# Transposing K and Q of the later batches with the DMA crossbar instead of TensorE, in a block-sparse attention and GELU kernel

## The chip, the cores and the metric

The kernel runs on one core of one Trainium2 chip. The metric is device time in microseconds (us) of one execution; medians are over the executions of one kernel on one chip. Each variant ran in the same rounds as the kernel before, on the same chip. A ratio is the mean time of one kernel's fast runs over the mean of the other's fast runs of the same rounds, so it is not quite the ratio of the medians that are quoted. Faster or slower needs 2%.

## The reference, cut to what matters

```python
# q, k, v: (4, 8, 768, 64) fp32; block 32, so 24 blocks; 3 sampled blocks for each query block
mask = |blk_i - blk_j| <= 1, or either of them the first or last block, or blk_j sampled for blk_i
attn = softmax(where(mask, q @ k.T / 8, -1e9)) @ v       # per batch and head
x = attn as (3072, 512)
out = gelu(x @ w_in) @ w_out                             # 512 -> 2048 -> 512, gelu with erf
```

Batch 0 computes dense scores with a mask; batches 1 to 3 gather sampled keys and values per query block.

## The kernel before

The work is a pipeline of half batches (384 rows each). In the stretch that I call a half, TensorE (PE) runs the hidden layer ("H" in the order strings) and the output layer ("O") of one half batch, and between them the scores ("S") and weighted sums ("W") of the next one. A fixed string of tokens gives the order of issue, and every engine takes its instructions in that order.

For batches 1 to 3, GpSimd's (Pool's) queue loads K and Q and converts them to bf16 on the way. TensorE transposes each head pair into PSUM, and VectorE (DVE) copies the result to SBUF:

```python
def load_qk(b, which, n):                       # four heads at once, bf16 tile
    t = st_pool.tile([P, NPAIR, NT * D], BF16, tag="st", name="st")
    pool.dma_start(out=t, in_=src[b, 4 * n:4 * n + 4].rearrange("h (p j) d -> p h (j d)", j=NT))

def transpose_qk(b, hp, which, pair, eng, st):  # 12 transposes, one copy
    dst = qkt_pool.tile([P, S], BF16, tag=f"t{which}", name=f"t{which}")
    ps = home[0].tile([P, NT, P], BF16, tag=home[1], name="ps")
    for j in range(NT):
        for h in range(2):
            pe.transpose(ps[64 * h:64 * h + 64, j, :], pair[:, h, j * D:j * D + D], ident)
    ...                                         # cuts: copy ps -> dst on VectorE
```

V is loaded in fp32 (batch 1 from Pool's queue, the others from SyncE's (SP's)) and cast by VectorE (`own_step`, token "B"). Then six SBUF-to-SBUF transfers on SyncE's queue move its blocks into four rotated copies (`rotate_all`, token "R"). Pool gathers the sampled values from these (`gather_v`, token "C", tile `v_gat`) and the sampled keys (`gather_k`, token "K", tile `kg_all`).

The softmax here doesn't subtract the row's maximum and nothing guards it: scores larger than these inputs give would overflow.

Of the kernel before, what the change touches and what calls it, by code (L numbers as in the profile page):

```python
# [19 lines left out]
P = 128  # L20
# [17 lines left out]
NROT, NULL, NAT1 = NT, NB, NB + 1  # L38
# [21 lines left out]
A0 F00 k1 F01 F02 q1 F03 F04 F05 k3 P0 F10 F11 F12 k2 q2 F13 J0 F14 F15 F20 V00 V01 V02 F21 J1 F22 q3 F23 F24 F25 X0 F30 V10 V11 V12 P1 F31 F32 J2 F33 X1 V20 V21 V22 J3 F34 M1 F35 X2 V30 V31 L1 V32 H X3"""  # L60
FIRST = """
H H m0 I0 m1 m2 I1 H H m3 m4 H I2 I3 H H I4 H O2 I5 O1 f00 O2 f01 m5 f02 O2 I6 I7 F03 F04 V00 O1 F05 f10 V01 O1 f11 V02 f12 f13 O2 f14 f15 O1 V10 O1 X0 F20 F21 u0 V11 V12 B F22 F23 V20 O1 t0 f24 f25 O1 X1 V21 O1 f30 F31 u1 V22 F32 O2 t1 f33 F34 O1 V30 f35 K00 X2 O1 I8 O1 V31 V32 Q0 O1 R Q1 H K01 X3 O2"""
SECOND = """
H t2 H u3 t3 C00 H C01 C02 H G H H H M2 H K02 O2 K03 S0 u2 K11 K10 C10 C11 O4 D0 O2 L2 W0 S1 O3 D1 X0 C12 O1 E0 W1 S2 O2 E1 O1 X1 K12 D2 O1 W2 S3 O2 X2 E2 D3 O1 W3 E3 O2 K13 Y X3 O3 H"""
SPARSE = """
H H Z H H B H O1 H H O1 H O2 S0 O1 t1 K01 O3 W0 S1 O1 t0 X0 O2 W1 u0 S2 X1 O1 K00 R O2 C00 O1 C01 C02 u1 W2 S3 O2 X2 O3 W3 H O2 X3 O2"""
DENSE = """
M3 H H t2 u2 H H H t3 u3 H H H O2 K03 K02 O1 L3 K10 S0 O1 C10 O2 D0 O1 G O1 W0 S1 O1 K12 O2 C11 D1 O1 X0 W1 C12 S2 O2 E0 K13 O1 D2 O1 E1 W2 S3 O1 K11 O1 X1 E2 D3 O1 W3 E3 O2 Y X2 O3 X3 H"""
SPARSE2 = """
H H Z H H B H O1 H H O1 H O2 S0 O1 t1 K01 O3 W0 S1 O1 t0 X0 O2 W1 u0 S2 X1 O1 K00 R O2 C00 O1 C01 C02 u1 W2 S3 O2 X2 O3 W3 H O2 X3 O2"""  # L70
DENSE2 = """
H H t2 u2 H H H t3 u3 H H H O2 K03 K02 O1 K10 S0 O1 C10 O2 D0 O1 G O1 W0 S1 O1 K12 O2 C11 D1 O1 X0 W1 C12 S2 O2 E0 K13 O1 D2 O1 E1 W2 S3 O1 K11 O1 X1 E2 D3 O1 W3 E3 O2 Y X2 O3 X3 H"""
LAST_SPARSE = """
H H H Z H O1 H H H H O2 S0 O5 S1 W0 O5 W1 S2 O1 X0 X1 O3 W2 S3 O4 X2 O1 W3 H X3 O2"""
LAST = """
H H H O2 H H O2 H H H O28"""
# [4 lines left out]
def kernel(  # L81
# [23 lines left out]
    sc_pool, og_pool, mm_pool = psum(opening, 0, (3, 1, 1))  # L105
    st_pool = ctx.enter_context(tc.tile_pool(name="st_pool", bufs=4))
# [21 lines left out]
    def load_v(b, eng):  # L128

        t = stv_pool.tile([P, NT, H, D], F32, tag="st_v", name="st_v")  # L130
        for n in range(NT):
            eng.dma_start(out=t[:, n], in_=v[b, :, n * P:n * P + P].rearrange("h p d -> p h d"))
        return t
# [51 lines left out]

    kg_all = small("kg_all", [2, NPAIR, NQH, P], BF16, const)
# [23 lines left out]
    qgl = [small(f"qgl{hp}", [P], BF16, const) for hp in range(NPAIR)]  # L210
    vgl = [small(f"vgl{i}", [NPAIR, 2 * VW], BF16, const) for i in range(2)]
    n_all = (NAT1 + NT) * H * GW
    v_flat = small("v_flat", [2 * -(-n_all // DW) * DW], BF16, const)
# [8 lines left out]
    pe.matmul(ps_raw, lhsT=ones, rhs=raw_b, start=True, stop=True)  # L222
    dve.tensor_copy(sbf.rearrange("p n s -> p (n s)"), ps_raw)
    dve.tensor_scalar(hit, sbf, key_b[:, 0:1], None, op0=ALU.is_equal)
    for s in range(NR):
        dve.tensor_add(seen, seen, hit[:, :, s])
    dve.tensor_scalar(barred.rearrange("p (n c) -> p n c", c=BLOCK),
                      seen.unsqueeze(2).to_broadcast([P, NB, BLOCK]),
                      0.5, -30000.0, op0=ALU.is_lt, op1=ALU.mult)
# [31 lines left out]
    dve.memset(v_own[0][:, :, :, D:2 * GW], 1.0)  # L261

    def first_own(hp):
        r = slice(2 * hp, 2 * hp + 2)
        dve.tensor_copy(v_own[0][:, :, r, 0:D],
                        first_v[:, r].rearrange("p h (j d) -> p j h d", d=D))

    def gather_constants():
        dve.tensor_copy(sbi, sbf)

        for n, (m, op) in enumerate(((15, ALU.bitwise_and), (7, ALU.bitwise_and),
                                     (8, ALU.bitwise_and), (5, ALU.arith_shift_right))):
            dve.tensor_single_scalar(lane_i[:, n:n + 1], part_i, m, op=op)
        dve.tensor_copy(lane, lane_i)
        dve.tensor_single_scalar(lane[:, 1:2], lane[:, 1:2], float(GW), op=ALU.mult)
        dve.tensor_single_scalar(lane[:, 2:3], lane[:, 2:3], 0.125, op=ALU.mult)
        for s in range(NR):
            dve.tensor_single_scalar(slotm[:, s:s + 1], lane[:, 3:4], float(s), op=ALU.is_equal)

        dve.tensor_scalar(mask_ka, mask_ka, lane[:, 0:1], None, op0=ALU.is_equal)  # L280
        dve.tensor_scalar(rowm, rowm, lane[:, 0:1], None, op0=ALU.is_equal)

        for h, picks in enumerate((((2, 1), (3, 0)), ((0, 8), (3, 13)))):
            (a0, add0), (a1, add1) = picks
            dve.tensor_scalar(base_k[:, h, :], cols, float(add0), rowm[:, a0:a0 + 1],
                              op0=ALU.add, op1=ALU.mult)
            dve.tensor_scalar(term, cols, float(add1), rowm[:, a1:a1 + 1],
                              op0=ALU.add, op1=ALU.mult)
            dve.tensor_add(base_k[:, h, :], base_k[:, h, :], term)
        dve.memset(v_flat[:, 2 * NULL * H * GW:2 * n_even * DW], 0.0)  # L290
        if 2 * n_all < v_flat.shape[1]:
            dve.memset(v_flat[:, 2 * n_all:], 0.0)
        dve.memset(v_own[1][:, :, :, D:2 * GW], 1.0)
# [58 lines left out]
    def value_indices(par, eng):  # L352

        if par:
            own = msk.tile([P, NQ], F32, name="own")
            eng.tensor_scalar(own, base_v, float(NROT) - 0.5, float(NAT1),
                              op0=ALU.is_lt, op1=ALU.mult)
            eng.tensor_add(base_v, base_v, own)
        for h in range(2):
            even = base_v[:, NQH * h:NQH * h + NQH:2]  # L360
            eng.tensor_sub(step, base_v[:, NQH * h + 1:NQH * h + NQH:2], even[:, 0:5])
            eng.tensor_copy(idx_vf[:, h, :], even)
            eng.tensor_scalar(step, step, lane[:, 2:3], None, op0=ALU.mult)
            eng.tensor_add(idx_vf[:, h, 0:5], idx_vf[:, h, 0:5], step)
        eng.tensor_scalar(idx_vf, idx_vf, float(H * GW), lane[:, 1:2], op0=ALU.mult, op1=ALU.add)
        eng.tensor_copy(idx_v[par], idx_vf)
# [22 lines left out]
    def own_v(b, st_v, lo, hi, eng):  # L389
        n = slice(lo, hi)  # L390
        cast(eng, v_own[b % 2][:, n, :, 0:D], st_v[:, n])
# [16 lines left out]
    def gather_v(b, hb, c):  # L408
# [3 lines left out]
            v_flat.bitcast(F32)[:, 0:n_even * DW if b % 2 == 0 else None]  # L412
# [21 lines left out]
    def globals_qk(b, hp, which, eng, st):  # L434
        gl = kgl[b % 2][hp] if which == "k" else qgl[hp]
        for i in range(2):
            rs = slice(64 * i, 64 * i + 64)
            cast(eng, gl[rs, rs].rearrange("p (n c) -> p n c", n=2),
                 st[which, hp][rs, :].rearrange("p (n c) -> p n c", c=BLOCK)[:, 0::NB - 1, :])
# [40 lines left out]
    def dense_scores(hp, st):  # L480

        pd = p_pool.tile([P, NT, P], BF16, tag="pd", name="pd")
        sd = sc_pool.tile([P, 2, 512], F32, tag="sc", name="sd")
        for t in range(NT):
            pe.matmul(sd[:, t // 3, t % 3 * P:t % 3 * P + P], lhsT=st["k", hp][:, t * P:t * P + P],
                      rhs=qgl[hp], start=True, stop=True)
        act.activation(pd.rearrange("p (a t) c -> p a (t c)", a=2), sd[:, :, 0:3 * P],
                       AF.Exp, scale=scale)
        st["pd", hp] = pd
# [89 lines left out]

    def pair_x(hb, hp, og, st):  # L580
# [26 lines left out]
    def hidden_steps(b, hb, st):  # L607
# [12 lines left out]
        def gelu(m):  # L620
            if m == 0:
                st["g", hb] = g_pool.tile([P, KOUT, HALF], BF16, tag="g", name="g")
            act.activation(st["g", hb][:, m:m + 2, :], held.pop(m)[:, :, 0:HALF], AF.Gelu)
# [5 lines left out]
        def step(m):  # L629
            mms(m, range(KIN - 1, KIN) if m < 4 else range(KIN))  # L630
            gelu(m)
# [35 lines left out]
    def first_pair(hp, which="kq"):  # L667
        for w in which:
            pair = st["st", w, hp // 2][:, 2 * (hp % 2):2 * (hp % 2) + 2, :]
            if hp == 0:  # L670
                cast(act if w == "k" else dve, pair, first_st[w])
# [5 lines left out]
    def load_batch(b):  # L677
        for n in range(2):
            for w in "kq":
                sts[b]["st", w, n] = load_qk(b, w, n)  # L680

    def transpose_next(b, hp, w):
        transpose_qk(b, hp, w, sts[b]["st", w, hp // 2][:, 2 * (hp % 2):2 * (hp % 2) + 2, :],
                     dve, sts[b])
        globals_qk(b, hp, w, pool, sts[b])
# [13 lines left out]
    def fetch_v(b):  # L699
        sts[b]["st", "v"] = load_v(b, pool if b == 1 else sp)  # L700

    def clear_keys():
        for t in kgl[0] + kgl[1] + qgl:
# [25 lines left out]
    def run(half, order):  # L729
# [5 lines left out]
        if nb < B:  # L735
# [19 lines left out]
            "t": lambda hp: transpose_next(b + 1, hp, "k"),  # L755
            "u": lambda hp: transpose_next(b + 1, hp, "q"),
# [5 lines left out]
            "L": lambda n: load_batch(n),  # L762
            "M": lambda n: fetch_v(n),
# [45 lines left out]
```

## Time and profile before

| | |
|---|---|
| time | 288.87 us, median of 3 runs (287.73 to 289.42); with the fourth run of the result's rounds 288.30 |
| profiled run | span 286.8 us, granted TensorE clock 1.0 |
| PE busy | 93% |
| all DMA queues | 49.9% of the 16 engines' time, see below |

To see where time goes, I cut each trace at the starts of ScalarE's (ACT's) table loads that precede the gelus of a half, as its timeline shows them. Before, in us: opening 29.6, then eight halves of 45.7, 27.4, 30.5, 32.2, 31.7, 33.0, 29.4 and 27.2.

### The profile page before, as it was taken

The numbers are of one execution on the slowest core, as the hardware profiler recorded it, in microseconds if no ns is written. First come the engines' busy times: TensorE is split into PE (matmuls) and PEld (weight loads), VectorE is DVE, ScalarE is ACT, GpSimd is POOL, SyncE is SP. The second block draws the span as 40 slices with busy tenths as digits, with TensorE's granted clock in tenths as the row PEclk, the third lists the DMA queues.
The fourth block names the chain that finished last, engine by engine and source line by source line (L and its number), as shares of the span: only waits on it lengthen the run. The fifth ranks groups of instructions, "written<-read, shape, count | busy, mean of one in ns | idle before, by whom it ended". The sixth has DMA issues, their size and how long they took to land.

```text
span 286.8 us, 7929 instructions
## 1 busy us (share of the span) xinstructions
PE 265.4 (93%) x3453; PEld 163.5 (57%) x3495; DVE 142.0 (50%) x375; ACT 162.5 (57%) x215; POOL 95.1 (33%) x134
## 2 busy tenths in 40 slices
PE   1999799999799999999999999999998999999995
PEld 1466454465456765566566755566555755565544
DVE  7255498898804670486325652465326560153002
ACT  3698558774367555744467635654466635845420
POOL 8400830013444336334273534231453333100000
PEclk9999999999999999999999999999999999999999
DMA  7999999209891003969580970088000100000101
GB/s 167 238 250 209 209 234 201 58 2 237 219 181 39 11 33 70 186 155 257 128 137 37 135 163 2 3 201 217 37 2 37 41 37 2 25 35 19 39 37 73
DMA packets 30036, 31.27 MB, mean 109 GB/s; under 512 B 13649, under 2 KB 24146, under 8 KB 30002
## 3 DMA queue, kind: packets, MB, share of 16 engines
q0 software_dynamic: 11936, 13.24, 26.5%
q1 hardware_dynamic: 18064, 17.53, 23.4%
q8 instruction: 27, 0.44, 0.6%
q14 instruction: 7, 0.06, 0.1%
q10 hardware_dynamic: 2, 0.00, 0.0%
HBM read 27.26 MB, written 6.29 MB: 117 GB/s over the span
## 4 chain that ended last, share of the span: by engine, by line
PE 60%; DVE 16%; issue 11%; POOL 7%; ACT 5%; POOLq 0%; DVEq 0%; ACTq 0%
PE hp L54 21%; PE op L54 18%; PE s L54 7%; PE og L54 6%; PE ps L54 4%; POOL kg_all L54 3%; POOL v_gat L54 2%; DVE v_flat L54 2%; PE psx L54 2%; DVE v_gat L54 1%; ACT L54 1%; ACT g L54 1%; POOL st L54 1%; PE od L54 1%; ACT kg_all L54 1%
## 5 line engine op out<-in xcount | busy, mean ns | idle before, releaser
L54 PE MATMUL op<-w_out_sb,g 128*128 128x512 bf16 (+1 forms) x358 | 89.8, 370 | 2.2 <-issue 0.2
L54 PE MATMUL hp<-xT,w_in_sb 128*128 128x384 bf16 x512 | 88.5, 326 | 2.9 <-ACT g L54 2.5
L54 ACT ACTIVATE g<-hp 128x768 bf16<-128x768 f32 x64 | 51.0, 810 | 61.1 <-PE hp L54 61.0
L54 PEld LDWEIGHTS <-w_in_sb 128*128 128x128 bf16 x512 | 49.1, 98 | 38.3 <-issue 5.2
L54 ACT ACTIVATE pt_all<-s 128x1024 bf16<-128x1024 f32 (+2 forms) x72 | 44.2, 687 | 30.4 <-PE s L54 30.3
L54 PEld LDWEIGHTS <-g 128*128 128x128 bf16 x400 | 35.6, 98 | 27.4 <-issue 1.6
L54 POOL INDIRECT_COPY kg_all<-tk,idx_k 128x704 f32 x24 | 30.3, 1262 | 58.8 <-issue 53.9
L54 DVE TENSOR_TENSOR pt_all<-pt_all,mask_x 128x768 bf16<-128x768 bf16 x24 | 14.7, 614 | 56.5 <-ACT pt_all L54 56.5
L54 POOL INDIRECT_COPY v_gat<-v_flat,idx_v 128x1024 f32 (+1 forms) x18 | 28.5, 1581 | 39.7 <-issue 16.4
L54 DVE COPY os<-op 128x512 f32<-128x512 f32 (+1 forms) x25 | 16.7, 667 | 21.5 <-PE op L54 20.9
L54 PEld LDWEIGHTS <-pt_all 128*32 128x32 bf16 (+2 forms) x818 | 22.0, 99 | 9.0 <-issue 2.9
L54 PE MATMUL s<-tq,tk 64*128 64x128 bf16 (+1 forms) x240 | 24.6, 272 | 1.2 <-DVE tq L54 0.7
L54 ACT ACT_TABLE_LOAD x16 | 20.5, 1283 | 8.0 <-PE hp L54 6.5
L54 PEld LDWEIGHTS <-tk 64*128 64x128 bf16 (+1 forms) x312 | 14.1, 96 | 14.0 <-issue 9.0
L54 PEld LDWEIGHTS <-st 128*64 128x64 bf16 x384 | 12.9, 118 | 14.1 <-issue 8.3
L54 ACT ACTIVATE kg_all<-s 128x768 bf16<-128x768 f32 x24 | 17.9, 814 | 4.9 <-PE s L54 4.9
L54 PE MATMUL ps<-ident,st 128*64 128x128 bf16 x384 | 17.4, 236 | 2.8 <-DVE st L54 1.4
L54 ACT ACTIVATE v_gat<-s 128x768 bf16<-128x768 f32 x24 | 18.1, 813 | 3.1 <-PE s L54 2.9
L54 DVE COPY tk<-ps 128x768 bf16<-128x768 bf16 (+1 forms) x16 | 13.4, 835 | 11.3 <-PE ps L54 11.2
L54 DVE TENSOR_TENSOR x<-og,rc 128x384 bf16<-128x384 f32 x32 | 17.8, 557 | 1.1
L54 DVE CAST v_flat<-st_v 128x1536 bf16<-128x1536 f32 (+1 forms) x10 | 8.9, 917 | 17.4 <-POOL v_gat L54 17.4
L54 DVE COPY tq<-ps 128x768 bf16<-128x768 bf16 (+1 forms) x16 | 14.8, 926 | 3.2 <-PE ps L54 3.2
(119 smaller groups left out, 244.7 us busy)
## 6 DMA issues: line engine op xcount, KB each, us to landing
out_dram<-os SPq DMA_DIRECT2D x23, 256.0 KB, 2.1
v_flat<-v_flat SPq DMA_DIRECT2D x6, 594.0 KB, 7.0
st_v<-in_v_dram SPq DMA_DIRECT2D x12, 256.0 KB, 4.9
st<-in_k_dram POOLq DMA_DIRECT2D x7, 384.0 KB, 7.2
st<-in_q_dram POOLq DMA_DIRECT2D x7, 384.0 KB, 8.4
v_flat<-v_flat SPq DMA_DIRECT2D x6, 396.0 KB, 5.2
w_in_sb<-in_moe_w_in_dram POOLq DMA_DIRECT2D x2, 1024.0 KB, 18.1
w_out_sb<-in_moe_w_out_dram POOLq DMA_DIRECT2D x2, 1024.0 KB, 26.7
```

Of the source, the lines that this page charges most:

```text
L54: return self._tc.keep_in_program_order(f(*args, **kwargs))
```

## The change

The intent is to take the transposes of K and Q away from TensorE, which is the bound, and give them to the DMA crossbar: a transfer (`dma_start_transpose`, DMA_TRANSPOSE in the profile) that writes its data transposed. The loads stay in fp32; VectorE casts a head pair into one of two bf16 buffers (`pr`), and SyncE's queue starts a transposing transfer from there. Loads of batch 1 are on Pool's queue, those of batches 2 and 3 on ACT's. The order strings are new (token "l" or "L" for a load, "t" or "u" for a cast with its crossbar transfer of K or Q, "M" for V; "F" or "f" is a set of scores of batch 0, "V" their weighted sums, "X" a pair of x turned on TensorE, "x" one turned by the crossbar, "g" small copies of K on Pool).

```diff
+    pr_pool = ctx.enter_context(tc.tile_pool(name="pr_pool", bufs=2))
+    def load_pair(b, which, hp):
+        t = sts[b]["st", which, hp] = st_pool.tile([P, 2 * NT, D], F32, tag="st", name="stf")
+        (pool if b == 1 else act).dma_start(
+            out=t, in_={"q": q, "k": k}[which][b, 2 * hp:2 * hp + 2].rearrange("h (j p) d -> p (h j) d", p=P))
...                                             # load_v likewise, four transfers of two heads
-    def transpose_next(b, hp, w):
-        transpose_qk(b, hp, w, ...)
-        globals_qk(b, hp, w, pool, sts[b])
+    def turn_pair(b, which, hp):
+        pair = pr_pool.tile([P, NT, P], BF16, tag="pr", name="pr")
+        dve.tensor_copy(pair.rearrange("p j (h d) -> p h j d", h=2),
+                        sts[b]["st", which, hp].rearrange("p (h j) d -> p h j d", h=2))
+        dst = sts[b][which, hp] = qkt_pool.tile([P, S], BF16, tag=f"t{which}", name=f"t{which}")
+        sp.dma_start_transpose(out=dst.rearrange("p (j n) -> p j n", j=NT), in_=pair.rearrange("p j c -> p (j c)"))
...                                             # four x pairs: turn_x, also on SyncE
...                                             # opening: 19 + 9 dummy matmuls, later mask, split cast of Q
...                                             # dense scores: 12 matmuls of half the rows and columns
```

## The prediction

> **What bounds the kernel now.** I read the page from the top. The busy rows come first, to see whether one engine is full all the time.
>
> ```profile
> PE 265.4 (93%) x3453; PEld 163.5 (57%) x3495; DVE 142.0 (50%) x375; ACT 162.5 (57%) x215; POOL 95.1 (33%) x134
> ...
> PE   1999799999799999999999999999998999999995
> ...
> DVE  7255498898804670486325652465326560153002
> ACT  3698558774367555744467635654466635845420
> ...
> DMA  7999999209891003969580970088000100000101
> ```
>
> One digit is 7.2 us. TensorE (PE) is at nine tenths nearly everywhere; the others are half full. The exceptions are the first 75 us: the opening (to about 31 us, scores and softmax of the first half batch) and the first half (to about 75 us), where VectorE (DVE) shows 8s and 9s and PE shows 7s. So after 75 us the time is PE's work, and before that a chain through several engines. The view of waits confirms it: ScalarE (ACT) waits for PE, hardly ever the other way.
>
> ```profile
> ACT g L54 <- PE hp L54: 61.0, 55, 4.5
> ...
> DVE tk L54 <- PE ps L54: 11.2, 7, 3.0
> ...
> PE hp L54 <- ACT g L54: 2.5, 5, 0.6
> ```
>
> (us in total, times, longest.) Next come the groups by form, for what the removed operations cost (busy us, mean ns of one).
>
> ```profile
> L54 PE MATMUL ps<-ident,st 128*64 128x128 bf16 x384 | 17.4, 236 | 2.8 <-DVE st L54 1.4 <-ACT st L54 0.7 <-DVE tk L54 0.2
> ...
> L54 DVE COPY tq<-ps 128x768 bf16<-128x768 bf16 x15 | 14.3, 950 | 2.5 <-PE ps L54 2.5
> L54 DVE COPY tk<-ps 128x768 bf16<-128x768 bf16 x15 | 13.1, 873 | 11.3 <-PE ps L54 11.2
> ...
> L54 DVE CAST v_flat<-st_v 128x768 bf16<-128x768 f32 x4 | 2.2, 550 | 0.0
> ```
>
> The mean of 236 ns is a latency of pipelined instructions, not what one transpose takes from PE. For that I use start-to-start times in PE's timeline in a dense stretch:
>
> ```profile
> 119.97 0.53 PE L54 MATMUL ps<-ident,st 128*64 128x128 bf16 x12
> 120.43 1.47 PE L54 MATMUL op<-w_out_sb,g 128*128 128x512 bf16 x6
> ...
> 124.33 0.34 PE L54 MATMUL psx<-ident,x 128*128 128x128 bf16 x3
> 124.51 1.03 PE L54 MATMUL op<-w_out_sb,g 128*128 128x512 bf16 x4
> ```
>
> Twelve transposes, that is one head pair of K or Q, take 120.43 - 119.97 = 0.46 us; three x transposes take 0.18 us. Last, the opening of the timeline:
>
> ```profile
> 9.22 0.81 ACT L54 ACTIVATE kg_all<-s 128x768 bf16<-128x768 f32 x1 [0.40 <-PE s L54]
> ...
> 10.52 0.53 PE L54 MATMUL s<-tq,tk 64*128 64x384 bf16 x2
> ...
> 10.84 0.53 PE L54 MATMUL s<-pt_all 64*128 64x384 bf16 x2
> ...
> 15.11 0.33 PE L54 MATMUL s<-tq,tk 64*128 64x384 bf16 x2
> ...
> 15.28 0.33 PE L54 MATMUL s<-pt_all 64*128 64x384 bf16 x2
> ```
>
> The same two matmuls take 10.84 - 10.52 = 0.32 us from start to start early on and 15.28 - 15.11 = 0.17 us later: PE runs at half rate until about 14 us, although the clock row shows 9 throughout. The first exponential starts at 9.22 us.
>
> **What the Trainium skill says.** "TensorE: Matmul & The Clock Gate", Part 1, says that the array runs at half clock until it has been busy for some 3.4 us; the pairs above agree with the factor of two, and the added warm-up matmuls aim at this. "VectorE: DVE Perf Modes", The three transpose paths, gives 390 ns for a 128x128 bf16 transpose on TensorE and 1309 ns through the DMA crossbar; the trace shows PE's as pipelined at 38 ns per half-width one, so the alone figure is not its cost here. "Advanced Engine Details and Errata", X-Bar Transpose (TRN2), says that transposing DMAs are as fast as ordinary ones; no transfer of the kernel before tests it. "DMA: Bandwidth & Descriptors", Issuing engines are not separate DMA queues, says that another issuing engine saves only sequencer time and that all transfers share 16 engines. So moving loads to ACT gains no bandwidth, and ACT now pays the issue.
>
> **The change, part by part.** (1) PE loses the transposes of K and Q of three batches: 3 x 4 pairs x 2 = 24 groups of 0.46 us = 11.0 us. About 20 groups lie after 75 us, in the PE-bound part, worth 9.2 us; four lie in the first half (1.8 us). (2) Four x pairs go through the crossbar: 4 x 0.18 = 0.7 us. (3) The dense scores become 12 matmuls of half the columns and half the rows instead of 6; the two heads use different rows of the array and can overlap, so about nothing. The hidden layer has the same matmuls. (4) VectorE: 24 copies out of PSUM of about 0.91 us (22 us) are replaced by 24 casts of 128x768 fp32 from SBUF, for which the 550 ns row stands: 13 us. It loses 9 us, three of the 14 mask products (0.6 us each) and four buffer clearings, which matters only in the first half, where it is nearly full. (5) GpSimd loses the small copies of global Q, off the path.
>
> (6) The opening: 19 + 9 dummy matmuls warm the clock while the first load is awaited, and the cast of Q is split between two engines. Before, PE needs twice 0.85 us for the first K and Q transposes at half rate and a further 0.5 us for the first scores, where it should need about half; the Q cast (0.73 us on VectorE after a long mask write) starts earlier. I take 2 us off the 9.22 us. Then 24 exponentials of 0.81 us are 19.4 us of ACT; their idle gaps while PE is cold add some 3 us, of which 2 go. Opening: -4 us. (7) The first half takes about 45 us against my sum of PE's start-to-start times of 37 us; less transposing there (1.8 us) and a lighter VectorE (about 4 us of its 36): -3 us.
>
> Sum without new costs: 9.2 + 0.7 + 4 + 3 = 17 us.
>
> (8) New costs. 24 fp32 loads of 384 KB are issued from ACT: eight in the second half batch, four in the third, eight and four again. The present queue issues of value loads are the nearest row (ns, minimum/median/maximum):
>
> ```profile
> L54 SPq DMA_DIRECT2D st_v<-in_v_dram x12: 426/944/1287, 76.2 to 143.8; - x12
> ```
>
> They have 1024 runs of 256 bytes; the new ones have 1536, so I estimate 0.6 to 1.4 us each, 14 to 34 us of ACT's queue. In the hidden layer ACT has little to spare:
>
> ```profile
> 80.24 0.81 ACT L54 ACTIVATE g<-hp 128x768 bf16<-128x768 f32 x1 [0.49 <-PE hp L54]
> 81.54 0.81 ACT L54 ACTIVATE g<-hp 128x768 bf16<-128x768 f32 x1 [0.49 <-PE hp L54]
> ```
>
> A step is 1.30 us and ACT idles 0.49 us of it, so one issue makes ACT late by about 0.5 us beyond that, and PE has to wait when its score buffers are full. The new order spreads output matmuls between and gives hidden steps 4 and 5 two further PSUM buffers, so I charge PE about 1.5 us for each half with eight loads and 1 us for each with four: 5 us. For latency and contention of 24 + 8 transposing transfers I add 0.5 us. Net gain: 17 - 5 - 0.5 = 11.5 to 12.5 us; I take 12.4: 288.9 - 12.4 = 276.5 us.
>
> **The rivals.** A: ACT becomes the bound of the halves with eight loads. Its work there is about 21 us of 31 (eight gelus 6.5, four score exponentials of 2.06 = 8.2, four dense ones 3.3, two table loads 2.6); eight issues of 1.3 us make it 31 us, as long as PE's. For it: the 944 ns median. Against: the 426 ns minimum, and that loads are spaced, so a queue that is full behind five others need not be met. It would cost some 4 us in each of two halves beyond my 5: about 284 us.
>
> B: the crossbar is slow and its results come late. Six tiles of the skill's 1309 ns would be 7.9 us a transfer, an estimate, and 24 of them 189 us on one queue that also carries outputs and the value rotations. Then keys would come late for the gathers and PE would wait. Against: the orders place the transfers some ten hidden or output steps (over 5 us) before their use, and the 256 KB outputs land after 2.1 us. It would make about 285 to 292 us.
>
> C: nothing new is waited for, and the opening gains its full half rate too: 17 us or a bit more, 270 to 272 us.
>
> **Range and chances.** C sets the low end at 270 us, A the high end at 284 us. The removed PE work is sure and lies where PE is full, so faster by over 2% (under 283.1 us) has 0.77; a mix of A and B that eats the gain down to within 2% has 0.18, and slower 0.05.
>
> **What would show it right or wrong.** In the profile after: no group of transposes with batch 1 to 3 in the steady part and PE's busy time lower (by 24 x 12 x 219 ns = 63 us of summed latency in its rows, less where they overlap); two PE matmuls of first scores 0.17 us apart from the first one on; the first exponential near 7.2 us and the first hidden matmul near 27 us instead of 30.6; the first half near 42 us; the later halves shorter by 1 to 2 us each. Step 8 is read in the issue times on ACT's queue and in PE's wait for the gelu, which I expect to grow from 2.5 to about 5 us. PE waiting on gathered keys, or transfers that take more than 6 us to land, would mean B. If the issues on ACT take over 1.4 us and halves with eight loads don't shrink, A.

## More of the kernel before

The prediction shows the busy rows, the waits and the groups. Two more views matter for what followed. The first is the chain of work that ended last (shares of the span by engine) and the DMA queues (packets, MB, share of the 16 engines' span) on the page of the kernel before:

```profile
q0 software_dynamic: 11936, 13.24, 26.5%
q1 hardware_dynamic: 18064, 17.53, 23.4%
...
PE 60%; DVE 16%; issue 11%; POOL 7%; ACT 5%; POOLq 0%; DVEq 0%; ACTq 0%
```

q0 is Pool's queue, q1 is SyncE's. Their shares add up to 49.9%, which is 143 us of all 16 engines. No transfer is on the chain. The second view is Pool's timeline (start, duration, what ended the idle time before); this is the first gather of values of batch 1:

```profile
81.16 1.66 POOL L54 INDIRECT_COPY v_gat<-v_flat,idx_v 128x1024 f32 x1 [2.17 <-issue]
```

It reads the rotated copies, so it can only start when all six rotations have landed.

## The result

The change made the kernel slower: 307.99 us median (305.77 to 311.08, 4 runs; the highest counts as slow), ratio 1.0657 with a 95% interval of 1.0541 to 1.0773. It is correct. Executions over 1.5% slower than the fastest of the same kernel are left out of the means.

The busy row of PE and the rows of slices on the page after (one digit is 7.6 us):

```profile
PE 266.5 (88%) x3301; PEld 158.3 (52%) x3301; DVE 135.5 (45%) x363; ACT 162.5 (53%) x224; POOL 90.3 (30%) x104
...
PE   7878999808997799939999799987999999998995
...
DVE  6445788447503456613641355614342561053002
...
PEclk9999999966999999968999999979799999999999
DMA  7999995597999911999383973999051100011002
```

PE's total is about what it was, although it lost 288 transposes: its row has holes, and beside the 0 and the 3 the clock row drops to 6. In the two longest stalls of this trace, from 60.59 and from 128.74 us on, the granted clock fell to 0.50 some 3 us after PE had stopped (it is 1.00 up to 63.6 and up to 131.8 us) and stayed there for some 4 to 5 us after PE went on at 69.96 and 133.91 us. Matmuls took longer there, so these stalls were paid for twice. DMA shows 9s over most of the first 210 us, where it had long gaps before. Three lines of the view of waits (us in total, times, longest), and the chain:

```profile
ACT g L54 <- PE hp L54: 52.6, 41, 6.0
...
DVE pr L54 <- DMA tk<-pr: 21.6, 5, 8.9
...
ACT g L54 <- DMA tq<-pr: 9.6, 2, 6.3
```

```profile
PE 55%; DMA 20%; DVE 12%; issue 4%; ACT 3%; ACTq 2%; SPq 1%; POOL 1%; DVEq 0%; POOLq 0%
```

ACT still mostly waits for PE, as before. New are waits for crossbar transfers: VectorE before its casts, and ACT before a gelu, which doesn't even read `tq`. (Pool waits for `tk` too, 9.1 us before small copies.) Transfers now make 20% of the chain.

Cut into halves, against before:

| us | opening | 1st | 2nd | 3rd | 4th | 5th | 6th | 7th | last | span |
|---|---|---|---|---|---|---|---|---|---|---|
| before | 29.6 | 45.7 | 27.4 | 30.5 | 32.2 | 31.7 | 33.0 | 29.4 | 27.2 | 286.8 |
| after | 28.1 | 54.2 | 31.1 | 36.0 | 32.4 | 34.3 | 31.9 | 27.1 | 29.1 | 304.3 |
| difference | -1.5 | +8.5 | +3.7 | +5.5 | +0.2 | +2.6 | -1.1 | -2.3 | +1.9 | +17.5 |

The loss has places. The largest is in the first half, at 60 to 70 us. Three lines of the timelines of SyncE's queue, VectorE and PE:

```profile
56.60 1.31 SPq L54 DMA_TRANSPOSE tk<-pr  x1
...
62.66 0.58 DVE L54 CAST pr<-stf 128x768 bf16<-128x768 f32 x1 [5.63 <-DMA tk<-pr]
...
69.96 0.50 PE L54 MATMUL psx<-ident,x 128*128 128x128 bf16 x3 [9.37 <-DVE x L54]
```

The first two casts fill both `pr` buffers. The third waits 5.63 us for the first crossbar transfer, which took from 56.60 to about 62.6 us: the loads that the first casts released had gone out at 56.86 and 57.87 us beside it. Behind the third cast, in VectorE's order, stand the fourth, the value casts and at last the normalisation of x that PE needs. PE is idle for 9.37 us and then runs at half clock: the granted clock is 0.50 from 65 to 70 us and 0.61 from 70 to 75 us.

The second place is ACT's queue. From its timeline and SyncE's, in the third half:

```profile
127.18 1.21 SPq L54 DMA_TRANSPOSE tq<-pr  x1
...
132.63 0.37 ACTq L54 DMA_DIRECT2D stf<-in_q_dram  x1
133.05 0.81 ACT L54 ACTIVATE g<-hp 128x768 bf16<-128x768 f32 x1 [6.33 <-DMA tq<-pr]
```

The gelu stands in ACT's order behind the issue of a load, and the load was held until the crossbar transfer, issued at 127.18 us on another queue, had landed. The instruction records of the packed trace show why. A completion semaphore is the counter by which a transfer tells that it has landed. The compiled program uses eight of them (100, 102, 103 and 114 to 118) in turn for the transfers of SyncE's and ACT's queues together. This load has 103, whose last user was that crossbar transfer; it landed at 132.55 us, and just before the load ACT has a wait for 103, which ends at 132.59 us. PE then waits 5.17 us for the gelu. In the second half it is the issue itself that is long, while many transfers are under way:

```profile
90.01 3.99 ACTq L54 DMA_DIRECT2D stf<-in_q_dram  x1
```

Last, the DMA queues of the page after (q10 is ACT's):

```profile
q1 hardware_dynamic: 26448, 19.46, 28.8%
q0 software_dynamic: 6464, 11.67, 18.8%
q10 hardware_dynamic: 37250, 9.44, 17.7%
```

These add up to 65.3% of 304.3 us, or 199 us of all 16 engines, against 143 us before. Packets under 512 bytes went from 13649 to 59185. By the packet records, 36864 of them are the loads on ACT's queue and some 19800 the crossbar transfers, all of 256 bytes; so the new loads, too, are made of small packets.

### The profile page after: what moved, and what is told of

It is laid out like the page before. It is cut to its first block, busy times and chain, and to the rows that moved or that the text cites. A ratio compares the mean times of both kernels' runs of the same rounds, so it can differ in the third digit from the quotient of the medians.

```text
span 304.3 us, 7659 instructions
## 1 busy us (share of the span) xinstructions
PE 266.5 (88%) x3301; PEld 158.3 (52%) x3301; DVE 135.5 (45%) x363; ACT 162.5 (53%) x224; POOL 90.3 (30%) x104
## 3 DMA queue, kind: packets, MB, share of 16 engines
q1 hardware_dynamic: 26448, 19.46, 28.8%
q10 hardware_dynamic: 37250, 9.44, 17.7%
## 4 chain that ended last, share of the span: by engine, by line
PE 55%; DMA 20%; DVE 12%; issue 4%; ACT 3%; ACTq 2%; SPq 1%; POOL 1%; DVEq 0%; POOLq 0%
PE op L54 20%; PE hp L54 18%; PE s L54 7%; DMA tq<-pr 7%; PE og L54 6%; DMA v_flat<-v_flat 4%; DMA st_v<-in_v_dram 4%; ACTq L54 2%; DMA xT<-x 2%; DVE v_flat L54 2%; ACT pt_all L54 2%; DMA tk<-pr 2%; PE psx L54 1%; DVE x L54 1%; SPq L54 1%
## 5 line engine op out<-in xcount | busy, mean ns | idle before, releaser
L54 PE MATMUL op<-w_out_sb,g 128*128 128x512 bf16 (+1 forms) x400 | 102.0, 387 | 0.0
L54 PE MATMUL hp<-xT,w_in_sb 128*128 128x384 bf16 x512 | 87.0, 326 | 2.0 <-DMA xT<-x 1.3
L54 ACT ACTIVATE g<-hp 128x768 bf16<-128x768 f32 (+1 forms) x72 | 50.7, 741 | 67.7 <-PE hp L54 52.6
L54 ACT ACTIVATE pt_all<-s 128x1024 bf16<-128x1024 f32 (+2 forms) x72 | 44.2, 687 | 30.3 <-PE s L54 23.4
L54 POOL INDIRECT_COPY v_gat<-v_flat,idx_v 128x1024 f32 (+1 forms) x18 | 31.7, 1763 | 57.0 <-issue 27.4
L54 DVE CAST pr<-stf 128x768 bf16<-128x768 f32 x24 | 18.0, 770 | 32.4 <-DMA tk<-pr 21.6
L54 PEld LDWEIGHTS <-tk 64*128 64x128 bf16 x384 | 12.5, 94 | 20.5 <-issue 16.3
L54 PEld LDWEIGHTS <-kg_all 64*128 64x128 bf16 (+1 forms) x672 | 15.5, 95 | 13.7 <-issue 11.7
L54 PE MATMUL psx<-ident,x 128*128 128x128 bf16 x84 | 9.5, 223 | 10.3 <-DVE x L54 10.2
L54 PE MATMUL s<-tq,kg_all 64*128 64x32 bf16 x528 | 10.5, 174 | 8.8 <-ACT g L54 7.7
L54 PEld LDWEIGHTS <-x 128*128 128x128 bf16 x84 | 6.3, 98 | 16.7 <-DVE x L54 12.4
## 6 DMA issues: line engine op xcount, KB each, us to landing
w_out_sb<-in_moe_w_out_dram POOLq DMA_DIRECT2D x2, 1024.0 KB, 26.8
```

The lines of the kernel that those rows point to most:

```text
L54: return self._tc.keep_in_program_order(f(*args, **kwargs))
```

## The experiments

I held three theories. B1: with two cast buffers, VectorE stops at the third cast until the first crossbar transfer has landed, and PE starves behind it. B2: loads on ACT's in-order queue hold up the gelus. B3: the crossbar transfers are too slow or too late whatever the buffers and queues. Each run shows what is changed against the changed kernel, unless said otherwise.

**1. pr3: three cast buffers.**

```diff
-    pr_pool = ctx.enter_context(tc.tile_pool(name="pr_pool", bufs=2))
+    pr_pool = ctx.enter_context(tc.tile_pool(name="pr_pool", bufs=3))
```

> Changed kernel with three instead of two cast buffers between VectorE and the crossbar. Theory B1 (VectorE stops at the third cast of a batch until the first crossbar transfer has landed, and TensorE starves behind it): the waits of VectorE casts on crossbar transfers fall from 28 us to under 12, the first half (54.2 us between table loads in the changed kernel) shrinks by 4 to 7 us, total about 300 us. Theory B2 (the loads on ScalarE's queue hold the gelus): no more than 2 us gained, about 306. Theory B3 (the crossbar transfers themselves and what shares the DMA engines come too late, whatever the buffers): the wait moves to the gathers or to the scores, about 306.

Measured: 296.14 us, ratio 1.0266 (1.0235 to 1.0297). VectorE's waits for crossbar transfers fell from 21.6 + 6.1 = 27.7 us to 13.5 us, PE's stall from 9.37 to 5.18 us. B1 is a real part, but not all, and the 12 us are not B1's alone: the first half shrank by 3.2 us (54.2 to 51.0, less than expected) and the third by 6.1 us (36.0 to 29.9), where the wait of 6.33 us on ACT's queue is gone. One edit moved both stalls.

**2. ld_pool: all loads on Pool's queue.**

```diff
-        (pool if b == 1 else act).dma_start(     # twice
+        pool.dma_start(
```

> Changed kernel with all fp32 loads on GpSimd's queue, none on ScalarE's. B2: the second, third and fifth halves (31.1, 36.0, 34.4 us) return to or below those of before (27.4, 30.5, 31.7), total about 295 us, and the waits of gelus and score exponentials on DMA and issue (about 21 us) vanish. B1: the first half stays at 54 us and the total is above 300. B3: loads land as late as before, total about 305 or more.

Measured: 316.23 us, ratio 1.0949. The second and third halves shrank, as B2 wants (31.1 to 28.7 and 36.0 to 30.1 us), and the first stayed (55.2 us), as B1 wants, but the fourth to sixth grew to 41.3, 37.1 and 37.2 us. Pool issues the loads between its gathers, in bunches, and a bunch delays whatever small transfer is under way. One line of PE's timeline:

```profile
153.66 2.74 PE L54 MATMUL hp<-xT,w_in_sb 128*128 128x384 bf16 x8 [8.93 <-DMA xT<-x]
```

Four loads of 384 KB went out between 136.99 and 141.55 us, and PE waited 8.93 us for an x crossbar transfer issued at about 142 us. Taking the loads off ACT helped the second and third halves; on Pool's queue, in this order, they cost more elsewhere.

**3. pe_turn: K and Q from the cast buffer back on TensorE.**

```diff
-        sp.dma_start_transpose(out=dst.rearrange("p (j n) -> p j n", j=NT), in_=pair.rearrange("p j c -> p (j c)"))
+        ps = mm_pool.tile([P, NT, P], BF16, tag="mm", name="ps")
+        for j in range(NT):
+            pe.transpose(ps[:, j, :], pair[:, j, :], ident)
+        dve.tensor_copy(dst.rearrange("p (j n) -> p j n", j=NT), ps)
```

> Changed kernel with its fp32 loads and orders, but K and Q of batches 1 to 3 transposed by TensorE from the cast buffer (six whole 128x128 transposes a pair) and copied out by VectorE; no crossbar for K and Q. B1 and B3: the first half falls to about 43 us and the total to 285 to 292 us, since nothing on VectorE waits for a transfer of the crossbar. B2: the halves with loads on ScalarE's queue stay 3 to 5 us longer than before, total 297 us or more.

Measured: 310.79 us, ratio 1.0768. This is a miss as a test: the orders were made for a transfer that no engine waits for, and now PE waits in its order for VectorE's casts (17.2 us in its weight loads, 12.0 us in the transposes); the first half is 61.5 us instead of the 43 expected. It tells the theories apart no further. It does give one number. SyncE's queue has 14.74 MB and 17.1% of 307.5 us, or 52.6 us, without the K and Q transfers, and 19.46 MB and 28.8% of 304.3 us, or 87.6 us, with them. So 24 crossbar transfers take (87.6 - 52.6) / 24 = 1.46 us each of all 16 engines, an estimate from two traces, at (19.46 - 14.74) MB / 35.0 us = 135 GB/s. It is rather high, as the other transfers of the queue were slower too in the changed kernel: by its packet records all 256-byte packets of this queue, which are the crossbar's with the eight small x transfers, took 34.0 us. The rest of the queue moves 14.74 MB / 52.6 us = 280 GB/s, but mostly in packets of 2048 and 6336 bytes. The loads on ACT's queue, in packets of 256 bytes like the crossbar's, move 9.44 MB / 53.9 us = 175 GB/s.

**4. x_pe: the four x pairs back on TensorE.**

```diff
-  ... X1 W2 x2 S3 ... / ... O1 x0 O1 Z O1 W1 S3 O1 x1 W2 ...
+  ... X1 W2 X2 S3 ... / ... O1 X0 O1 Z O1 W1 S3 O1 X1 W2 ...
```

> Changed kernel with the four x pairs transposed by TensorE again. If their crossbar transfers are harmless: within 1 us of the changed kernel. If they delay the next hidden layer (the trace of the changed kernel shows 1.3 us of TensorE waiting on them, and a last half 1.9 us longer than before): 2 to 4 us faster, about 304 us, with the gain in the seventh and eighth halves.

Measured: 307.08 us, ratio 1.0629, no difference from 1.0657. The last half went from 29.1 to 27.8 us; the rest hid it. Experiment 9 comes back to this.

**5 and 6. pr4 and pr4_sp: four cast buffers; and then also the loads of batches 2 and 3 on SyncE's queue.** SBUF is full, so room is made by giving two small tiles one buffer and letting two others share one.

```diff
+    pr_pool = ctx.enter_context(tc.tile_pool(name="pr_pool", bufs=4))     # pr4
-        (pool if b == 1 else act).dma_start(                              # pr4_sp, twice
+        (pool if b == 1 else sp).dma_start(
```

> Changed kernel with four cast buffers instead of two (three gave 296 us). Room for it comes from single instead of double xd and xdT tiles and one scratch tile used twice. B1: the casts of a batch no longer wait for a transfer at all, waits of casts on the crossbar fall from 13.5 us (three buffers) to under 3 us, the first half falls from 51.0 to 46 us or less, total 286 to 292 us. B2: most of the loss left lies in the second and fifth to sixth halves and stays: total about 294 us. B3: the waits move to the gathers and scores: 294 us or more.

> Four cast buffers, and the loads of batches 2 and 3 issued on SyncE's queue instead of ScalarE's. B2: ScalarE's waits of gelus and exponentials on DMA and issue (some 15 us in the three-buffer run and in the changed kernel) vanish, 3 to 8 us faster than four buffers alone. Against B2: the loads then hold the crossbar transfers and outputs on SyncE's queue and nothing is gained, or up to 5 us is lost.

Measured: pr4 305.18 us, ratio 1.0521 (1.0434 to 1.0608), a miss: four buffers are worse than three. Its runs spread from 300.68 to 309.12 us, two of the four count as slow (so the ratio rests on two), and the profiled one is one of these, so I read only its mechanism. ACT's timeline and PE's:

```profile
68.37 16.25 ACTq L54 DMA_DIRECT2D st_v<-in_v_dram  x2
...
86.86 3.36 PE L54 MATMUL hp<-xT,w_in_sb 128*128 128x384 bf16 x10 [12.13 <-ACT g L54]
```

VectorE no longer waits, so the rotations go out on SyncE's queue at 65.64 us, six in 12.30 us, and now the two value loads keep ACT's queue for 16.25 us. The stall moved from VectorE to ACT, and PE waits 12.13 us for a gelu. The second of the two loads took 15.81 us by itself. The last user of its completion semaphore, a crossbar transfer, had landed at 67.12 us, before this issue began at 68.80 us, as far as the trace pairs landings with issues. So in this profile the semaphore is not what held it; what did is not shown. With the loads on SyncE, pr4_sp takes 290.37 us, ratio 1.0122 (1.0061 to 1.0183), and the first half is 45.3 us, as before the change. Both edits seem to be needed for the first half, as the next run shows.

**7. pr2_sp: two cast buffers, loads on SyncE's queue.** This completes a square.

> The changed kernel with only one edit: the loads of batches 2 and 3 are issued by SyncE instead of ScalarE; two cast buffers as in the change. With the runs of four cast buffers this makes a square of two by two. B1 and B2 as separate causes that each reach the chain: the two edits are not additive, because either one alone leaves the other stall. Four buffers alone gave 1.4% less (1.066 to 1.052), both gave 1.012. If the ACT queue (B2) is the larger cause, this run is near 1.03 (297 us), and ACT's waits for DMA (ACT g <- DMA tq<-pr, 18 us in total) go while VectorE's cast waits (some 27 us in total) stay. If B1 alone sets the time when the buffers are two, it is 1.05 to 1.07 (303 to 308 us), the first half stays at about 54 us.

Measured: 295.35 us, ratio 1.0257 (1.0209 to 1.0305). ACT's waits for `tq` are gone (9.6 us in the changed kernel, not the 18 us of the expectation), VectorE's casts still wait 15.9 us for `tk` and 3.0 us for `tq`. The second, third and fifth halves fell from 31.1, 36.0 and 34.3 to 26.8, 28.8 and 28.4 us, so the loads on ACT had cost some 4, 7 and 6 us there; the fourth grew to 37.1 us, where PE now waits for an x transfer. PE's timeline:

```profile
68.61 0.50 PE L54 MATMUL psx<-ident,x 128*128 128x128 bf16 x3 [9.05 <-DVE x L54]
...
144.56 5.62 PE L54 MATMUL hp<-xT,w_in_sb 128*128 128x384 bf16 x25 [5.32 <-DMA xT<-x]
```

| ratio (first half, us) | loads on ACT | loads on SyncE |
|---|---|---|
| two cast buffers | 1.066 (54.2) | 1.026 (53.1) |
| four cast buffers | 1.052 (56.8, a slow run) | 1.012 (45.3) |

I had expected that the two edits would not add up. In the whole time they do (ratio down by 1.4 and 4.0 per cent alone, 5.4 together), within the noise, as the interval of pr4 alone is 0.9 to either side. In the first half they don't seem to: of the four profiled runs only the one with both has it repaired. Each of these is a single trace, and that of pr4 is of a slow run.

**8. pr4_noload: as pr4, without any K, Q or V loads for batches 2 and 3,** which compute on batch 1's data. The result is wrong.

```diff
+        if b > 1:
+            sts[b]["st", which, hp] = sts[1]["st", which, 2 + hp % 2]
+            return
```

> Four cast buffers, and no loads of K, Q and V for batches 2 and 3: their casts read again what batch 1 left, so the result is wrong on purpose. Crossbar transfers, casts and orders stay. B3 with B2: without loads beside them the crossbar transfers land in about 2.7 us instead of a median of 4 to 5 and a maximum of 8 to 10 in batches 2 and 3, the issues on ScalarE vanish, and the halves from the second on fall to about 27 to 31 us each, total 275 to 280 us. If the crossbar is slow by itself: landing times stay and the total is within 3 us of four buffers with loads.

Measured: 284.68 us, ratio 0.9866 (0.9824 to 0.9907), some 19 us less than pr4 by the ratios, but above the 275 to 280 us expected; crossbar transfers of K and Q landed after 3.0 and 3.8 us (medians), not 2.7. So with 24 loads fewer the loss of pr4 is gone, but the crossbar version is still only 1.3% below the time before, the same by the 2% rule: the loads are not all of it. The second half is still 34.5 us against 27.4, with PE waiting 3.37 and 2.54 us for value gathers. The only loads of K, Q and V left there are those of batch 1, so that part of the loss is in batch 1's own transfers.

**9. pr4_sp_x: pr4_sp with the x pairs on TensorE,** by the same edit of the orders as in experiment 4.

> Four cast buffers, loads of batches 2 and 3 on SyncE, and the four x pairs back on TensorE. If the x crossbar transfers are a part of what remains, the last half loses 1 to 1.5 us (28.9 to about 27.5), the waits PE hp <- DMA xT<-x (6.1 us) go, and the ratio falls from 1.012 to about 1.00 (285 to 288 us). If they are harmless, as the run of the whole change with x on TensorE showed (no gain), it stays at 1.01.

Measured: 284.69 us, ratio 0.9860 (0.9811 to 0.9910), better than expected. The waits of PE for `xT` (6.1 us in matmuls and 5.5 us in weight loads in pr4_sp) are gone. Small x transfers queued on SyncE behind larger ones were harmful here and hidden in experiment 4, where other stalls came first. What remains is the wait for value gathers in the second half. Pool's timeline of this run has the first gather of values. Below it are the six rotations in this run's timeline of SyncE, and then rotations and first gather in pr4_sp_late (experiment 11):

```profile
87.35 1.65 POOL L54 INDIRECT_COPY v_gat<-v_flat,idx_v 128x1024 f32 x1 [11.80 <-DVE pt_all L54]
```

```profile
63.97 4.14 SPq L54 DMA_DIRECT2D v_flat<-v_flat  x6
```

```profile
63.92 6.80 SPq L54 DMA_DIRECT2D v_flat<-v_flat  x6
...
81.52 1.65 POOL L54 INDIRECT_COPY v_gat<-v_flat,idx_v 128x1024 f32 x1 [3.27 <-DVE pr L54]
```

**10. pr4_sp_early: pr4_sp_x with the first four casts, their crossbar transfers and the last four loads of batch 1 earlier in the first half.**

```diff
-  O1 V00 F05 f10 ... X0 t0 u0 F20 F21 t1 u1 l02 l12 V10 V11 B g0 l03 l13 V12
+  O1 t0 u0 l02 l12 V00 F05 t1 u1 l03 l13 f10 ... X0 F20 F21 V10 V11 B g0 V12
```

> As the run before, and in the first half the first four casts with their crossbar transfers and the last four loads of batch 1 come some 15 us earlier, so that they don't meet the value rotations. If the collision of these loads with the rotations is what makes the second half 33 us instead of 27.4, the second half falls to 28 to 30 us, the first value gather starts near 76 to 80 us instead of 85, and the whole is 281 to 285 us (ratio 0.98 to 0.99). If VectorE, full in the first half, pays for the earlier casts, the first half grows by 2 to 3 us and the sum stays at 1.00.

Measured: 285.00 us, ratio 0.9896 (0.9857 to 0.9936), no gain on run 9. The first gather came at 83.96 us (76 to 80 expected) and the second half fell from 35.0 to 31.6 us, but the first half grew from 45.4 to 46.8 us: VectorE, busy with the earlier casts, lets PE wait 2.81 us for a normalised x from 52.17 us on. Both parts of the expectation came half true. The two traces don't carry the whole difference: this one is of the fastest of its runs and that of run 9 of the slowest, and its opening, by the same code, is 26.7 us against 28.1.

**11. pr4_sp_late: pr4_sp_x with those four loads behind the rotations** and the casts of pairs 2 and 3 and batch 2's value loads later in the second half, behind the first value gather or more.

```diff
-  F20 F21 t1 u1 l02 l12 V10 V11 B g0 l03 l13 V12 ... R ... Q0 K01
+  F20 F21 t1 u1 V10 V11 B g0 V12 ... R ... Q0 l02 l12 K01 l03 l13
-  t2 C00 u2 G M0 C01 M1 C02 u3 g2 t3 H H H g3 M2 H H K02
+  C00 G C01 t2 C02 u2 H H H t3 g2 u3 M0 M1 H H M2 g3 K02
```

> Four cast buffers, loads of batches 2 and 3 on SyncE, x pairs on TensorE (ratio 0.986), and in batch 1 alone the last four key and query loads go out after the six value rotations instead of before them, with the casts and crossbar transfers of pairs 2 and 3 and the value loads of batch 2 behind the value gathers. In the run without this, the first value gather started at 87.35 us (before: 81.16) and TensorE waited 3.77 and 2.50 us for two gathers. If the rotations were late because these loads and crossbar transfers share the DMA engines with them, the first gather starts at 81 to 83 us, the waits of PE for v_gat shrink below 2 us, and the time is 279 to 283 us (ratio 0.97 to 0.98). If the engines' total work is what counts, the delay only moves to the keys of pairs 2 and 3 (their gathers, PE waiting on kg_all), and the ratio stays at 0.98 to 0.99.

Measured: 282.66 us, ratio 0.9748 (0.9701 to 0.9796), correct. This beats both kernels: 2.5% faster than before. The first gather is at 81.52 us, as in the kernel before, although the rotations were issued no earlier than in run 9 (63.92 and 63.97 us, lines above): what had made them land late was the traffic beside them. Whether it was more the loads or more the crossbar transfers is not separated. One of PE's two waits is left:

```profile
91.40 0.41 PE L54 MATMUL og<-v_gat,pt_all 128*32 128x65 bf16 x14 [2.64 <-POOL v_gat L54]
```

I had expected it below 2 us. The delay has partly moved: a cast of pair 2 now waits 3.74 us for its load. The second half is 31.5 us, still 4.1 us above before. The busy times by half account for it: PE is idle 3.5 us of it instead of 0.6, 2.64 us in the wait above, and busy 28.0 us instead of 26.8, at a mean granted clock of 0.89.

**12. before_open: the kernel before with the new opening alone** (dummy matmuls, split cast of Q, later mask, a reduction in place of three additions). Against the kernel before, cut:

```diff
+    warm_up(19)                                # 19 matmuls of the identity, and 9 later
...
-                cast(act if w == "k" else dve, pair, first_st[w])
+                act.copy(pair[:, 0:2 if w == "k" else 1], first_st[w][:, 0:2 if w == "k" else 1])
+            dve.tensor_copy(st["st", "q", 0][:, 1], first_st["q"][:, 1])
+            bar()                              # the mask, written after the cast
```

> The kernel before with only the opening of the change: 28 warm-up matmuls and the split cast of the first Q pair, the mask written after it. The opening (29.6 us between start and the first gelu table load) should fall to about 28 us as in the changed kernel, the other halves stay: 286 to 287.5 us, 0.5 to 1% faster than before.

Measured: 288.12 us, ratio 1.0023 (0.9996 to 1.0049): the same. The opening is 27.7 instead of 29.6 us in the trace, but the time does not show it.

All halves side by side (us; the clock is the mean granted clock of the profiled run):

| | opening | 1st | 2nd | 3rd | 4th | 5th | 6th | 7th | last | clock |
|---|---|---|---|---|---|---|---|---|---|---|
| before | 29.6 | 45.7 | 27.4 | 30.5 | 32.2 | 31.7 | 33.0 | 29.4 | 27.2 | 1.0 |
| after | 28.1 | 54.2 | 31.1 | 36.0 | 32.4 | 34.3 | 31.9 | 27.1 | 29.1 | 0.961 |
| pr4_sp | 27.7 | 45.3 | 33.3 | 28.4 | 33.4 | 28.4 | 33.0 | 27.1 | 28.9 | 0.987 |
| pr4_sp_x | 28.1 | 45.4 | 35.0 | 29.7 | 30.2 | 30.6 | 30.3 | 27.3 | 27.8 | 0.986 |
| pr4_sp_late | 28.5 | 44.9 | 31.5 | 29.7 | 30.8 | 30.7 | 30.2 | 27.3 | 27.8 | 0.988 |

Each row is one run: that of pr4_sp was the fastest of its four (287.36 us, median 290.37), those of pr4_sp_x and pr4_sp_late the slowest of theirs.

## Why the prediction was wrong

The prediction was 276.5 us, in 270 to 284, with 0.05 for slower; the result is 308 us. Its own terms give a gain of 17 - 5 - 0.5 = 11.5 us, or 277.4 us; that it took 12.4 has no reason in the text. Its steps:

- **Step 1, the removed transposes (9.2 us where PE is the bound): right in kind, and visible once little else waits.** The transposes of PE went from 384 to 96 in the trace. The third to sixth halves lost 16 of the 24 groups, 16 x 0.46 = 7.4 us by the prediction. In pr4_sp_late they are together 30.5 - 29.7 + 32.2 - 30.8 + 31.7 - 30.7 + 33.0 - 30.2 = 6.0 us shorter than before. That fits, but no run isolates it, as the orders changed too: the seventh half is 2.1 us shorter without having had any such transposes (no `ps` matmul after 230 us in the trace before), about half of it idle time of PE that is gone (1.0 us before, none here). In the changed kernel only the sixth half shows a gain of this kind (-1.1 us); no loads are made in it.
- **Step 2, x pairs (0.7 us): wrong in sign.** On the crossbar they cost 1.3 us in the last half (experiment 4), and with the other stalls gone the ratio was 1.0122 with them there and 0.9860 without.
- **Step 3, dense scores (about nothing), and step 5, Pool: right.** In PE's timeline one set of dense scores takes 0.28 us from start to start instead of 0.33, 0.6 us over all twelve; Pool's busy time went from 95.1 to 90.3 us, and no wait shows it.
- **Step 4, VectorE: the cast was mis-sized.** I took 550 ns from a row of the same size; the mean is 770 ns, with a median of 600 and single casts of up to 2030 ns. The own-step cast of V, which reads the new layout, went from 1161 to 1740 ns, which I had not looked at; two of these stand in the stall of the first half.
- **Step 6, the opening (-4 us): the mechanism was right, the size wrong.** The first two pairs of score matmuls are 0.16 us apart, so the clock is full from the start:

```profile
6.77 0.34 PE L54 MATMUL s<-tq,tk 64*128 64x384 bf16 x2 [0.67 <-DVE tq L54]
6.93 0.34 PE L54 MATMUL s<-pt_all 64*128 64x384 bf16 x2
```

  The first exponential is at 7.31 us (predicted 7.2), but the first hidden matmul at 28.91 us instead of 27: 1.9 us of lead at the start became 1.5 us of opening. Alone it moved the time by nothing that could be measured.
- **Step 7, the first half (-3 us): wrong even without stalls.** Where PE has no long stall in it, in pr4_sp and pr4_sp_late, it is 0.4 to 0.8 us shorter.
- **Step 8, the new costs (5.5 us): this is the step that failed.** I charged ACT for the time of its issues only, and 0.5 us for "latency and contention of 24 + 8 transposing transfers". PE's waits for a gelu were to grow from 2.5 to about 5 us; they are 9.3 us before scores and 0.6 us before hidden matmuls. The runs show three terms in place of the 5.5 us. First, the cast buffers: my argument against rival B was that the transfers are placed well ahead of their use. That is true of the reader of `tk`, but the writer of `pr` has two buffers, and in VectorE's order the third cast brings its wait for the crossbar to all that follows. In all, VectorE's casts waited 27.7 us, and PE 9.37 us behind those in the first half. A third buffer alone took 3.9 per cent off the ratio, some 11 us, though not by this stall alone (experiment 1). Second, ACT's queue: a load there waited for an earlier transfer of SyncE's queue, up to 6.33 us, and not only the 0.6 to 1.4 us charged for its issue, which itself went up to 3.99 us. Moving the loads to SyncE took 4.0 per cent off the ratio, some 11.5 us, with two buffers and with four. Third, contention: the DMA engines had 56 us more to do, at most 35 us of it for the crossbar (estimate above) and most of the rest for the loads in small packets, which my sum left out. The first gather of values came 6.2 us late in pr4_sp_x, whose first half has no long stall, and on time in pr4_sp_late, where the traffic beside the rotations had been moved away.
- **Rival B was nearest in kind:** late transfers, PE waiting. But keys were not late for the gathers as it says; the writers' buffers, the issue order of ACT and the values were. Its 285 to 292 us was still too low, and its 7.9 us for a transfer was not met: the medians to landing are 3.5 us (`tk`) and 5.1 us (`tq`). Rival A, ACT with too much to issue, was right in part. It counted 10.4 us for eight issues; the eight between 77 and 104 us took 10.9 us and the eight between 154 and 176 us took 10.1 us. Eight of the 24 took over 1.4 us, its sign. In the second half it fits: 3.7 us longer, and 4.3 us shorter again with the loads on SyncE (experiment 7). In the fourth it doesn't: only 0.2 us longer. And the 6.33 us in the third half are a wait for a landing, not the time of an issue.

What stays open: why four cast buffers with loads on ACT are worse than three, beyond that the stall moved. What held the value load on ACT's queue in pr4 is not shown either, beyond that it was not its semaphore. No run keeps the old loads with the crossbar, or the new loads in larger packets, so how the contention divides between the crossbar and the new layout of the loads is not shown. In pr4_sp_late the DMA share is still 0.98 or more in 65 to 85 us and again in 90 to 105 us.

## What to carry to other kernels

Moving work from a full engine to DMA paid here only once the engines that feed and issue the transfers could run on without them, and then 2.5% instead of the 4.3% predicted: count the buffers that the writer fills before the first transfer lands, and don't issue loads from the in-order queue of an engine that the critical path passes through. Before such a change, add up what the new transfers take of the 16 DMA engines in the stretches where they lie, not only whether each has time to land. When several stalls lie over each other, as here, undoing one alone may show no gain, move the stall or remove another one with it, so test them in pairs.

## What the Trainium skill lacked or had wrong

- "Advanced Engine Details and Errata", X-Bar Transpose (TRN2), has transposing DMAs as fast as ordinary ones. Against ordinary packets of the same size this nearly holds: in the changed kernel the median 256-byte packet took 18 ns on SyncE's queue, where they are all the crossbar's, and 18 ns on ACT's queue, where they are loads; the means are 27.4 and 23.2 ns. Against a queue's larger packets it does not: some 135 GB/s of engine time, an estimate from two traces, against 280 GB/s (experiment 3). The section gives no time for the issue: each of the 24 took 1.21 to 2.40 us of SyncE's queue. The median time to landing of `tk` and `tq` was 3.5 and 5.1 us in the changed kernel and 2.8 us for both in pr4_sp_late.
- "DMA: Bandwidth & Descriptors", Issuing engines are not separate DMA queues, says that initiating DMAs on several engines only saves the sequencer's time, which is usually small. That all share 16 engines agrees: the rotations on SyncE's queue landed late beside traffic that other queues had started too (first gather at 87.35 us against 81.52 without it, experiments 9 and 11). But the time on the sequencer was 0.37 to 3.99 us for the same kind of load on ACT, and the choice of queue moved the time by 4% (experiments 5 to 7).
- No page has that the compiled program gives the transfers of two engines' queues common completion semaphores, so that a load on ACT's queue can wait for the landing of SyncE's transfer; one did here, and a gelu behind it waited 6.33 us.
